# DeltaNet with a quick-GELU block: conversion steps, hops, Gram products and combinations of w_out in another order

## The chip, the cores and the metric

The kernel runs on one core of a Trainium2 chip. Its time is the device time of one execution in microseconds; the median of three runs is given. The engines are TensorE (PE, with its weight loads as PEld), VectorE (DVE), ScalarE (ACT), GpSimd (POOL) and SyncE (SP), whose queue issues most transfers. Each engine has its own instruction queue.

## The reference

```python
batch, n_heads, seq, head_dim = (4, 8, 768, 48)
n_tokens, d_model, d_ff = (3072, 384, 2048)

k_n = k / (np.linalg.norm(k, axis=-1, keepdims=True) + 1e-06)
state = np.zeros((B, H, D, D), dtype=np.float32)
for t in range(S):
    kt, vt, bt = (k_n[:, :, t], v[:, :, t], beta[:, :, t, None])
    y[:, :, t] = np.einsum('bhd,bhde->bhe', q[:, :, t], state)
    v_old = np.einsum('bhde,bhd->bhe', state, kt)
    state = state + bt[:, :, :, None] * np.einsum('bhd,bhe->bhde', kt, vt - v_old)

x = y.transpose(0, 2, 1, 3).reshape(B * S, H * D)
h = x @ w_in
g = h * (1.0 / (1.0 + np.exp(-1.702 * h)))
out = g @ w_out
```

`w_in` and `w_out` arrive as 64-bit floats; the kernel reads them as pairs of 32-bit words and makes 32-bit floats of them itself.

## The kernel before

**Units and chunks.** The sequence is cut into 6 chunks of 128 positions. A unit is one chunk of one batch with its 8 heads, so there are 24 units, numbered chunk by chunk: units 0 to 3 are chunk 0, units 4 to 7 (B to B + 3) chunk 1. Two units with the same chunk make a pair with one tile xT of 256 columns.

**A unit's own work.** For each unit the keys are normalized and transposed (`turn`, tile kT; psT is its PSUM tile), multiplied with themselves (`gram`, psG, tile G), and the diagonal blocks of 32 by 32 are sent through DRAM (`send_blocks`: tile Nd; `load_diagonal`: tile NT), so that one DVE routine, `invert`, inverts those of a whole chunk at once. The inverse comes back through DRAM as XB. Then the four blocks of a unit are solved one after another. `together` does one step of this for two units, a *hop*: for one unit `solve` (psU from XB and V on PE, copied by ACT to US), for the other `below` (psR from US and G on PE) and `rest`, in which DVE subtracts psR from V. A unit's next solve needs that subtraction, so hops alternate between PE, ACT and DVE. `queries`, `outputs` and `state` then make the unit's results (psY) and its new state ST; `put_out` calls them, copies psY to xT with ACT, and for the second unit of a pair moves the rows kept in `last` into xT by six transfers.

**Conversion.** `conversion` turns one piece of the 64-bit words into floats in five steps: a DVE step (`ts` on the high words) with an ACT step behind it, then a sign step, a step on the high words, a step on the low words and a product. `background()` strings all of them together: the 9 pieces of w_in, then `invert(1)`, the inverse of chunk 1, and then the 14 pieces of w_out, 23 pieces in all. `fill(us)` takes the next steps of this string, by costs written in the code, until the amount is used up. When a piece is done, `fetches` may start the load of a later one into the room that came free: the end of the second piece starts the last quarter of w_in (12 transfers), the end of the fourth starts w_out 4 to 7.

**Order.** Most instructions go through `pinned`, which keeps them in the order in which the program emits them, per engine and in SP's queue. Calls of `nc.gpsimd` and `nc.sync` that aren't pinned may be placed by the planner where the engine is free in its own estimate.

**Start of the program** (lines 1041 to 1187). Chunk 0's keys and inverse come first, then the masks of units 0 to 3 (`select`, POOL), then eight hops of units 0 and 1 with `fill(1.7)` behind each but the first, the Gram products of units 6 and 7 and their transfers, `put_out` of units 0 and 1, a list of transfers (the third, fourth and later loads of keys, the first three w_out pieces by `fetch_out`), then eight hops of units 2 and 3 with `fill(1.7)`, from the fourth on with a `feed()` each. `feed()` emits one step of `hidden`: three matmuls of x with w_in, or the last three of a pair of rows and the GELU on ACT (psum tile ph, result gT). After `put_out` of units 2 and 3, 25 rounds of `fill(1.0)` and `feed()` follow, in which `hidden` of the first two pairs ends.

**Main part.** `woven(n, share)` runs for each unit n from 3 on: solves for it, its follower and its forerunner, the preparation of a later unit (`normalize`, `prepare`), steps of a later inverse, and between them `spend`, which takes matmuls from a queue of FFN work. For the first pair that work is `both_written`, for the second `written`, and from the third on `hidden` and then `seven`, which multiplies gT with w_out by seven products of half size in place of eight. For that, four combinations of the quarters of w_out are needed:

```python
W11, W21 = w_out[:, 0:HF, 0:HM], w_out[:, HF:, 0:HM]
W12, W22 = w_out[:, 0:HF, HM:], w_out[:, HF:, HM:]
for o, a, b in ((T1, W12, W11), (T2, W22, T1), (T3, W22, W12), (T4, W21, T2)):
    for f in range(0, HF, n):
        add(o[:, f : f + n], a[:, f : f + n], b[:, f : f + n], sub_)
```

Each is four subtractions on POOL of 128 by 384 elements; `combined()` yields after each, 16 times. T3 takes the place of W12. T1, T2 and T4 lie in a tile TW of 4608 columns, 1536 each. Earlier TW holds other things: columns 0 to 2047 the later half of the second pair's gT (`late_g`, read by `written`), 2048 to 3071 queries of units 2 and 3 and then the mask of unit 5, 3072 to 3583 the keys KX of units 7 and 11, copied away in `follow(5)`. `follow(6)` queues `hidden` of the third pair, and `beside_of` takes one step of `combined()` before each of its 16 steps.

**Two rows that the prediction uses by name.** "rn" is the inverse key norm in `normalize`: POOL squares the keys (ksq), DVE sums them, POOL takes the root (rn), DVE adds a constant and inverts, POOL multiplies the keys (KN). The transposition of those keys (psT) is pinned in PE's order.

Of the kernel before, what the change touches and what calls it, by code (L numbers as in the profile page):

```python
# [18 lines left out]
def kernel(  # L19
# [21 lines left out]
    B, H, S, D = q.shape  # L41
# [9 lines left out]
    NB = C // BS  # L51
    HB = 2
    NTH = HB * C
    FQ = 4
    GB = 6
    HF, HM = FC // 2, DM // 2
# [22 lines left out]
    TW = cpool.tile([128, 3 * HF * HM], F32, name="TW")  # L79
# [10 lines left out]
    def load(n, pairs, dma=nc.sync.dma_start):  # L90
        c, b = units[n]
        for dst, src in pairs:
            dma(  # L93
                out=place(dst, n)[:, :, 0:D],
                in_=src[b, :, c * C : (c + 1) * C, :].rearrange("h p d -> p h d"),
            )

    def load_values(n, dma=nc.sync.dma_start):
        c, b = units[n]
        V = io.tile([128, H, D], F32, tag="V", name="V", bufs=4)  # L100
        dma(
            out=V, in_=v[b, :, c * C : (c + 1) * C, :].rearrange("h p d -> p h d")
        )
        loaded[n] = V
# [199 lines left out]
    def fill(us):  # L304
        while us > 0:
            us -= next(behind, us)
# [105 lines left out]
    def gram(n):  # L412

        c, b = units[n]
        kT = kTs[n]
        G = wk.tile([128, H, 128], F32, tag="G", name="G", bufs=6)
        pool_, tag = (ps_seq, "seq") if c == 0 else (ps_big, "big")
        ps = [pool_.tile([128, NP, 128], F32, tag=tag, name="psG") for _ in range(2)]
        for h in range(H):
            r = slice(h % 2 * 64, h % 2 * 64 + D)  # L420
            pe.matmul(
                ps[h % 2][:, h // 2], lhsT=kT[r, h // 2, :], rhs=kT[r, h // 2, :],
                start=True, stop=True,
            )
        act.activation(G[:, 0::2], ps[0], ACT.Copy)
        if B <= n < 2 * B + HB:
            act.activation(G[:, 1::2], ps[1], ACT.Copy)
        else:
            vec.tensor_copy(G[:, 1::2], ps[1])
        ready[n] = KN[n % len(KN)], kT, G  # L430
        return G
# [15 lines left out]
    def prepare(n):  # L447

        turn(n)
        yield 0.6  # L450
        gram(n)
        dma = sync if n < 3 * B else nc.sync.dma_start
        load_diagonal(n, send_blocks(n, dma=dma), dma)
        yield 0.9
# [6 lines left out]
    def send_blocks(n, others=(), dma=sync):  # L461

        G = ready[n][2]
        Nd = dram.tile([H * C * BS], F32, tag="Nd", name="Nd", bufs=4)
        to = Nd.rearrange("(h p k) -> p h k", p=C, k=BS)
        for blk in range(NB):
            u = slice(blk * BS, (blk + 1) * BS)
            (beside if blk in others else dma)(out=to[u], in_=G[u, :, u])
        return Nd

    def load_diagonals(Nds):

        for b in range(B):
            load_diagonal(b, Nds[b], sync)
# [90 lines left out]
    def bank(name, shape=(128, H, D)):  # L565
        return ps_seq.tile(list(shape), F32, tag="seq", name=name)
# [194 lines left out]
    def add(o, a, b, op, engine=None):  # L761
        (engine or nc.gpsimd).tensor_tensor(o, a, b, op=op)  # L762
# [1 line left out]
    W11, W21 = w_out[:, 0:HF, 0:HM], w_out[:, HF:, 0:HM]  # L764
    W12, W22 = w_out[:, 0:HF, HM:], w_out[:, HF:, HM:]
    T1, T2, T4 = (
        TW[:, i * HF * HM : (i + 1) * HF * HM].rearrange("p (f d) -> p f d", f=HF) for i in range(3)
    )
    T3 = W12

    def combined():

        n = 2
# [3 lines that stand above are left out]
                yield  # L777

    def beside_of(work, other):

        for cost in work:
            next(other, None)
            yield cost
        run(other)

# [108 lines left out]
    def take(cost):  # L894

        while cost > 0 and queue:
            more = next(queue[0], None)
            if more is None:
                queue.pop(0)
            else:  # L900
                cost -= more
                yield more

    def run(work):
        for _ in work:
            pass

    def ahead_of(work, n):
        for _ in range(n):
            next(work, None)  # L910
# [18 lines left out]
    def together(solves, belows):  # L929

        solves = [(X, blk) for X, blk in solves if X]
        belows = [(X, blk) for X, blk in belows if X]
        psU = bank("psU") if solves else None
        psR = bank("psR") if belows else None
        for h in range(H):
            for X, blk in solves:
                X.solve(blk, h, psU)
            for X, blk in belows:
                X.below(blk, h, psR)
        for X, blk in solves:  # L940
            X.solved(blk, psU)
        for X, blk in belows:
            X.rest(blk, psR)

    def follow(n):

        if n + 3 < len(units):
            load(n + 3, ((QP, q),))
        m = n - 1 + len(KN)
        if n == B + 1:  # L950
            nc.sync.dma_start(out=KN[m % len(KN)], in_=KX)
        elif n > B and m < len(units):
            load(m, ((KN, k),), nc.gpsimd.dma_start)
        if n - 1 + B < len(units):
            load_values(n - 1 + B)
        if n % HB == 0 and n > B:
            h = (n - 1) // HB
            gT, sums = [], []
            work = hidden(xTs[h], gT, slice(0, NTH), 1.3, sums)
            queue.append(beside_of(work, combined()) if h == HB else work)  # L960
            queue.append(seven(*units[h * HB], gT, sums))
            xTs.pop(h)

    debt = [0.0]

    def spend(cost):

        debt[0] = debt[0] + cost if queue else 0.0
        for done in take(debt[0]):
            debt[0] -= done  # L970
# [4 lines left out]
    def woven(n, share):  # L975

        nonlocal inverting  # L980
        A, B_, D_ = steps.pop(n - 1, None), steps.get(n), steps.get(n + 1) or NoStep()
        m = n + B + 1 if n > B else len(units)
        K = normalize(m) if m < len(units) and m >= 3 * B else iter(())
        P = prepare(m) if m < len(units) else iter(())
        if n == B:
            inverting = invert(*units[2 * B], HB)
        if n % HB == 1 and B + 1 < n and n + 1 + HB < len(units):
            inverting = invert(*units[n + 1 + HB], HB)
        ahead = FIRST[n] if n in FIRST else STEPS[:3] if n % HB == 1 else STEPS[3:]

        next(K, None)
        together([(B_, 1)], [(A, 2)])
        run(D_.scored)
        next(K, None)
        ahead_of(inverting, ahead[0])
        spend(share / 3)

        together([(A, 3), (D_, 0)], [(B_, 1)])
        next(K, None)
        ahead_of(inverting, ahead[1])  # L1000
        spend(share / 6)
        next(P, None)
        spend(share / 6)

        together([(B_, 2)], [(D_, 0)])
        if A:
            A.queries()
            A.outputs(True)
        run(P)
        ahead_of(inverting, ahead[2])  # L1010
        if n % HB == 0 and n > B:
            run(inverting)
        spend(share / 6)
        next(new_step(n + 2).scored, None)
        spend(share / 6)
        follow(n)

    queue = []
# [53 lines left out]
    pair = [new_step(n) for n in range(B)]  # L1072
# [11 lines left out]
    Ndx = [send_blocks(n) for n in (B, B + 1)]  # L1084
    run(scaling)
    pool.memset(late_U[:, H * D :], 0.0)
    for s in pair:
        s.select()

    def hops(a, b):  # L1090

        yield [(a, 0)], []
        for blk in range(NB - 1):
            yield [(b, blk)], [(a, blk)]
            yield [(a, blk + 1)], [(b, blk)]
        yield [(b, NB - 1)], []

    def put_out(s):
        s.queries()
        s.outputs(True, lambda: fill(1.7))  # L1100
        steps.pop(s.n)

    path = hops(*pair[:2])
    for i in range(2 * NB):
# [2 lines left out]
            turn(B + HB + i // 2)  # L1107
        if i > 0:
            fill(1.7)
    for n in (B + 2, B + 3):  # L1110
        gram(n)
        Ndx.append(send_blocks(n))
    load_diagonals(Ndx)
    for s in pair[:2]:
        put_out(s)
    sync(out=KN[0], in_=KX)
    load(8, ((KN, k),), sync)
    for f in range(3):
# [6 lines left out]
    def feed(n=1):  # L1125
        for _ in range(n):
            while ffn and next(ffn[0], None) is None:
                ffn.pop(0)

    gTs = [], []  # L1130
    ffn.append(hidden(xTs[0], gTs[0], slice(0, NTH), 1.3))
    path = hops(*pair[2:])
    for i in range(2 * NB):
        together(*next(path))
        if i > 2:
            feed()
        fill(1.7)
    for s in pair[2:]:
        put_out(s)
        feed()  # L1140
# [43 lines left out]
    queue = [both_written(0, gTs[0]), written(*units[HB], gTs[1])]  # L1184
# [34 lines left out]
```

## Time and profile before

| what | us |
|---|---|
| median of three runs | 775.18 (773.53 to 778.63) |
| the profiled execution's time | 778.5 |
| its span, first to last instruction | 776.8 |
| PE busy | 730.6 |
| DVE busy | 487.7 |
| ACT busy | 238.6 |
| POOL busy | 237.7 |

The profile is of one execution. All positions in this document are microseconds from the span's start. Most of the kernel's lines go through one helper, `pinned`, so nearly all rows carry its line number L108; they are told apart by tile names, "out<-in". "x4" is the number of instructions that a row merges. A bracket at a row's end is the engine's idle time before it and what ended it. PE's matmuls in 32-bit floats are two instructions each. In the table of busy shares by stretch, the stages around the edits read:

```profile
102.00:118.00 16.00, 16.00 (x200) 12.24 (x194) 12.58 (x25) 6.56 (x11) 0.00 (x0) 0.74 0.60 153
118.00:161.00 43.00, 42.61 (x263) 36.53 (x258) 40.75 (x87) 19.02 (x41) 8.12 (x5) 1.00 0.47 95
161.00:178.70 17.70, 14.09 (x99) 8.22 (x98) 16.26 (x34) 5.84 (x11) 0.00 (x0) 0.90 0.50 136
178.70:235.00 56.30, 55.51 (x789) 37.15 (x789) 44.22 (x94) 19.45 (x47) 14.01 (x13) 1.00 0.18 42
235.00:252.00 17.00, 12.45 (x119) 9.97 (x116) 13.34 (x32) 4.53 (x10) 12.18 (x11) 0.95 0.43 91
```

The columns are the stretch, its length, the busy time of PE, PEld, DVE, ACT and POOL with the number of instructions, the clock granted to PE as a share of the full one, the share of the transfer engines and GB/s. From 260 us to the end PE is busy almost without a break.

### The profile page before, as it was taken

What the parts mean: (1) busy time and instruction counts of PE and PEld (TensorE: products, weight loads), DVE (VectorE), ACT (ScalarE), POOL (GpSimd) and SP (SyncE); (2) the same over time, 40 slices, a digit from 0 to 9 for tenths busy, and PEclk for the clock granted to TensorE, in tenths of its full rate; (3) what the DMA queues carried; (4) which work ended last, traced back from release to release, by engine and by line L of the source; (5) the groups of instructions that cost most, each with busy time, mean ns of one, the idle gap of its engine ahead of it and who ended that gap; (6) DMA issues with size and microseconds to landing.
All of it is one profiled execution on the core that took longest, in us unless ns stands there. A gap on an engine that the chain in (4) does not pass through costs nothing.

```text
span 776.8 us, 19495 instructions
## 1 busy us (share of the span) xinstructions
PE 730.6 (94%) x8356; PEld 626.8 (81%) x8356; DVE 487.7 (63%) x1013; ACT 238.6 (31%) x527; POOL 237.7 (31%) x210
## 2 busy tenths in 40 slices
PE   8388789989997999999999999999999999999998
PEld 6266668856666898898898898888988988988988
DVE  4796689999768577687687687677677750120000
ACT  3363443533332322422323322322322313222120
POOL 5022001200057362352442542542620611403123
PEclk8576679999999899999999999999999999999999
DMA  9994654531224104104113113113113020000000
GB/s 169 123 173 100 169 127 82 123 102 50 59 46 84 35 13 95 38 19 92 35 25 84 35 27 84 35 31 79 36 23 77 20 56 2 2 27 1 26 1 21
DMA packets 128182, 47.11 MB, mean 61 GB/s; under 512 B 117920, under 2 KB 122144, under 8 KB 128096
## 3 DMA queue, kind: packets, MB, share of 16 engines
q1 hardware_dynamic: 125568, 41.54, 25.7%
q0 software_dynamic: 1344, 3.93, 2.2%
q8 instruction: 66, 1.08, 0.6%
q10 hardware_dynamic: 1184, 0.39, 0.2%
q14 instruction: 20, 0.16, 0.1%
HBM read 33.13 MB, written 11.01 MB: 57 GB/s over the span
## 4 chain that ended last, share of the span: by engine, by line
PE 74%; DVE 15%; DMA 4%; issue 3%; SPq 2%; POOL 2%; ACT 1%; DVEq 0%; POOLq 0%; ACTq 0%
PE ph L108 28%; PE po L108 25%; PE psY L108 5%; PE psU L108 5%; DVE P L108 4%; PE psG L108 4%; PE psQ L108 3%; DVE YB L108 3%; DVE w_out L108 2%; SPq L108 2%; PE psT L108 2%; PE psR L108 2%; DVE NT L108 2%; DMA w_out<-in_moe_w_in_dram 1%; DMA Nd<-G 1%
## 5 line engine op out<-in xcount | busy, mean ns | idle before, releaser
L108 PE MATMUL ph<-xT,w_in 128*128 128x256 f32 x1152 | 266.7, 387 | 0.4 <-DMA xT<-last 0.4
L108 PEld LDWEIGHTS ph<-xT,w_in 128*128 128x128 f32 x1152 | 217.6, 193 | 33.1 <-DVE V L108 1.4
L108 PE MATMUL po<-w_out,gT 128*128 128x192 f32 (+1 forms) x736 | 147.2, 354 | 4.0 <-DVE o L108 3.6
L762 POOL TENSOR_TENSOR gT<-gT 128x512 f32<-128x512 f32 x80 | 105.9, 1332 | 123.9 <-ACT gT L108 113.4
L108 DVE TENSOR_TENSOR V<-V,psR 64x384 f32<-64x384 f32 (+1 forms) x96 | 53.3, 556 | 135.5 <-PE psR L108 134.2
L108 PEld LDWEIGHTS po<-w_out,gT 128*128 128x128 f32 x736 | 121.2, 191 | 19.6 <-DVE o L108 4.6
L108 ACT ACTIVATE gT<-ph 128x512 f32<-128x512 f32 x92 | 54.9, 596 | 147.0 <-PE ph L108 146.9
L108 DVE TENSOR_TENSOR P<-NT,YB 64x2 f32<-64x2 f32 (+9 forms) x200 | 96.0, 480 | 6.2
L108 PEld LDWEIGHTS psU<-V,XB 32*32 32x32 f32 x1536 | 61.3, 109 | 33.6 <-issue 12.8
L108 DVE TENSOR_REDUCE YB<-P 64x2 f32<-64x2 f32 (+9 forms) x200 | 81.8, 409 | 6.9
L108 PE MATMUL po<-TW,gT 128*128 128x192 f32 x480 | 83.0, 328 | 0.0
L108 ACT COPY US<-psU 32x384 f32<-32x384 f32 x92 | 43.2, 469 | 128.5 <-PE psR L108 117.5
L108 PE MATMUL psU<-V,XB 32*32 32x48 f32 x1536 | 72.4, 208 | 9.4 <-DVE V L108 9.2
L108 PEld LDWEIGHTS po<-TW,gT 128*128 128x128 f32 x480 | 77.9, 190 | 1.1 <-issue 0.3
L108 PE MATMUL psR<-US,G 32*32 32x48 f32 x2208 | 63.7, 207 | 4.2 <-ACT US L108 4.1
L108 DVE TENSOR_TENSOR o<-o,po 128x192 f32<-128x192 f32 x40 | 13.5, 351 | 75.8 <-PE po L108 75.3
L108 PEld LDWEIGHTS psR<-US,G 32*32 32x32 f32 x2208 | 54.0, 108 | 5.6 <-ACT US L108 4.9
L631 POOL TENSOR_SCALAR_AFFINE_SELECT M<-M 128x1024 f32<-128x1024 f32 x19 | 22.3, 1173 | 94.3 <-DVE M L108 62.4
L108 DVE TENSOR_TENSOR P<-NT 64x512 f32<-64x512 f32 (+7 forms) x50 | 44.1, 883 | 2.4 <-DVE NT L108 0.5
L108 PE MATMUL psG<-kT 48*128 48x128 f32 x384 | 36.3, 335 | 1.3 <-ACT G L108 1.0
L93 POOL DMA_DIRECT2D KN<-in_k_dram x12 | 11.5, 958 | 84.1 <-PE psY L108 84.1
L108 PE MATMUL psQ<-QS,kT 48*128 48x176 f32 (+1 forms) x368 | 34.5, 330 | 0.8 <-ACT QS L108 0.8
(118 smaller groups left out, 735.7 us busy)
## 6 DMA issues: line engine op xcount, KB each, us to landing
V<-in_v_dram SPq DMA_DIRECT2D x24, 192.0 KB, 3.1
out_dram<-o SPq DMA_DIRECT2D x24, 192.0 KB, 2.1
QP<-in_q_dram SPq DMA_DIRECT2D x22, 192.0 KB, 3.3
raw<-in_moe_w_out_dram SPq DMA_DIRECT2D x9, 384.0 KB, 4.3
NT<-Nd SPq DMA_DIRECT2D x24, 128.0 KB, 2.9
XB<-Yd SPq DMA_DIRECT2D x24, 128.0 KB, 2.9
Nd<-G SPq DMA_DIRECT2D x92, 32.0 KB, 1.8
Yd<-NT SPq DMA_DIRECT2D x22, 128.0 KB, 2.2
```

Of the source, the lines that this page charges most:

```text
L93: dma(out=place(dst, n)[:, :, 0:D], in_=src[b, :, c * C : (c + 1) * C, :].rearrange("h p d -> p h d"),)
L108: return lambda *a, **kw: tc.keep_in_program_order(op(*a, **kw))
L631: (pool if self.n < B else nc.gpsimd).affine_select(out=self.M, in_=self.M, compare_op=ALU.is_gt, fill=0.0, base=0, pattern=[[0, H], [1, 1 ...
L762: (engine or nc.gpsimd).tensor_tensor(o, a, b, op=op)
```

## The change

Four edits. The areas of T1 and T4 in TW change places, and T1's four subtractions are emitted in `woven(6)`, while those of T2, T3 and T4 stay beside the fifth and later steps of `hidden`. `fill(5.5)` comes between the masks of chunk 0 and its first hop. The first two hops of units 2 and 3 move up: each is followed by `fill(1.0)`, the Gram product of unit 6 or 7 with its transfers, `put_out` of unit 0 or 1 and another `fill(1.0)`; the loads of the diagonals now come behind all of this. The other six hops of units 2 and 3 have `fill(2.3)` instead of `fill(1.7)`; feeds begin at the same hop as before.

```diff
     T1, T2, T4 = (
-        TW[:, i * HF * HM : (i + 1) * HF * HM].rearrange("p (f d) -> p f d", f=HF) for i in range(3)
+        TW[:, i * HF * HM : (i + 1) * HF * HM].rearrange("p (f d) -> p f d", f=HF) for i in (2, 1, 0)
     )
...
     def beside_of(work, other):
 
-        for cost in work:
-            next(other, None)
+        for i, cost in enumerate(work):
+            if i >= FQ:
+                next(other, None)
             yield cost
         run(other)
...
-            queue.append(beside_of(work, combined()) if h == HB else work)
+            queue.append(beside_of(work, combining) if h == HB else work)
...
+    combining = combined()
     debt = [0.0]
...
         next(P, None)
+        if n == B + HB:
+            ahead_of(combining, HF // 2)
         spend(share / 6)
...
     for s in pair:
         s.select()
+    fill(5.5)
...
-    for n in (B + 2, B + 3):
-        gram(n)
-        Ndx.append(send_blocks(n))
+    path = hops(*pair[2:])
+    for i in range(HB):
+        together(*next(path))
+        fill(1.0)
+        gram(B + HB + i)
+        Ndx.append(send_blocks(B + HB + i))
+        put_out(pair[i])
+        fill(1.0)
     load_diagonals(Ndx)
-    for s in pair[:2]:
-        put_out(s)
     sync(out=KN[0], in_=KX)
     load(8, ((KN, k),), sync)
     for f in range(3):
         fetch_out(f)
...
-    path = hops(*pair[2:])
-    for i in range(2 * NB):
+    for i in range(HB, 2 * NB):
         together(*next(path))
-        if i > 2:
+        if i > HB:
             feed()
-        fill(1.7)
+        fill(2.3)
```

`put_out` contains a fill of its own, between the products of the new state and the addition to ST:

```python
def put_out(s):
    s.queries()
    s.outputs(True, lambda: fill(1.7))
    steps.pop(s.n)
```

## The prediction

> **What bounds the kernel now.** I read the busy slices of the page first, then the timelines of VectorE (DVE), SyncE's queue (SP), GpSimd (POOL) and TensorE (PE) around the edited places, last the chain of waits from 234 us on. The slices (19.4 us each):
>
> ```profile
> PE   8388789989997999999999999999999999999998
> DVE  4796689999768577687687687677677750120000
> PEclk8576679999999899999999999999999999999999
> ```
>
> PE is near full from 110 us on and DVE until 190 us; both are loose between 60 and 110 us, and later PE itself dips in the thirteenth slice and its clock in the fourteenth (233 to 272 us). The edits touch just these two places. DVE's timeline of the first:
>
> ```profile
> 61.99 0.55 DVE L108 TENSOR_TENSOR TW<-TW 128x384 f32<-128x384 f32 x1
> 69.08 1.14 DVE L108 TENSOR_TENSOR V<-V,psR 32x384 f32<-32x384 f32 x2 [6.54 <-PE psR L108]
> ...
> 93.28 0.36 DVE L108 TENSOR_TENSOR ST<-psY,ST 128x192 f32<-128x192 f32 x1 [5.24 <-PE psY L108]
> ...
> 111.91 0.34 DVE L108 TENSOR_SCALAR w_out<-raw 128x384 int32<-128x384 int32 x1
> ```
>
> Two holes, 6.54 and 5.24 us, are to be filled. The last line is the first step of the first w_out piece; what it reads comes late in SP's queue:
>
> ```profile
> 94.37 1.80 SPq L108 DMA_DIRECT2D NT<-Nd  x4
> 96.22 4.94 SPq L108 DMA_DIRECT2D xT<-last  x6
> 101.26 0.54 SPq L108 DMA_DIRECT2D KN<-TW  x1
> 101.90 0.54 SPq L108 DMA_DIRECT2D KN<-in_k_dram  x1
> 102.49 1.65 SPq L108 DMA_DIRECT2D raw<-in_moe_w_out_dram  x3
> ```
>
> ```profile
> DMA to landing us min/median/max: 4.0/4.5/5.2
> ```
>
> So raw lands at 102.5 + 4.5 = 107, 5 us before DVE asks. The second place, first POOL's timeline, then the chain of waits:
>
> ```profile
> 223.76 1.68 POOL L762 TENSOR_TENSOR TW<-w_out 128x384 f32<-128x384 f32 x1 [3.74 <-PE po L108]
> ```
>
> ```profile
> 239.54 5.80 POOL TW L762 x5
> 245.34 1.05 POOL M L631
> 246.39 1.63 POOL rn L325
> 248.01 2.65 issue
> 250.70 1.01 POOL KN L329
> 251.76 1.11 PE psT L108 x4
> 252.88 6.00 PE ph L108 x18
> ```
>
> POOL's first combination waits 3.74 us for PE to read the TW area it overwrites; the 16 combinations end at 245.3, and the key normalization behind them holds PE for 4.19 us (its idle time before that psT). The 18 ph instructions then take 6.00 us, against 3.89 for 18 at 266.1: the clock has fallen to half.
>
> **Steps behind the masks.** Going through the costs of the generators, `fill(5.5)` emits seven steps. Priced by the starts of the same kinds at 70.2 to 76.6 (0.61, 0.59, 0.94, 1.83 for two, 0.61, 0.68) they are 5.3 us: 62.5 to 67.8, inside the first hole. The seventh also queues a 0.94 us ACT step (row at 71.55) ahead of the first hop's copy of U. That copy ran at 67.62; it now starts at about 68.8, and the hops 1.2 us later. The second piece's end releases twelve fetches of the last w_in quarter; SP reaches them behind the eight Nd stores at 71.9 instead of 74.6. DVE wants them at 88; hidden. The w_out fetches 4 to 7 follow the second quarter's end likewise, some 6 us sooner, and nobody waits.
>
> **Pair 1's first sets between Gram products and outputs.** DVE's work on chunk 0's first eight hops is the same 17 steps, on smaller pieces (512 for 768 columns), until about 86.7. Then fills of 1.0, 1.7 and 1.0 stand around each Gram product and output; the second hole is gone. PE's work is the one it had. In after's order I get, with PE at half clock: Gram 6 until 89, outputs of unit 0 until 92, first receiving hop 94, Gram 7 until 95.5, outputs of unit 1 until 98.5, next hop's subtractions until 101.6. Before, the same subtractions ended at 101.1. So the hops are not sooner, but DVE has eight more steps behind it (0.69, 0.95, 0.6, 0.6, 0.94, 0.92, 0.91, 0.61 = 6.2 us).
>
> **The new wait.** The next step in after's order, at once after those subtractions, is the first w_out step, which stood three hops later. Its fetch did not move up: in SP's queue it now stands behind the four stores of Gram 7, the six xT moves, the four NT loads and the two KN moves. Gram 7's copies wait on ACT behind a conversion step until 98.4; then four stores (1.8 at 160.6, 2.9 as half of eight at 88.4) to 100.2 to 101.3; six xT moves 3.7 (124.1) to 4.94; four NT 1.8; KN twice 0.6. The raw fetch goes at 107 to 109 and lands 4.0 to 4.5 later: 111 to 113, I take 112. (The NT loads land by 109, and the inverse needs them at 115: hidden, as long as raw is later.) DVE stands from 101.6 to 112, 10 us, and queued behind it are the subtractions of four hops, so PE stands too. The w_out step starts when it did before (111.9), but with hops 4 to 7 and their five feeds of `hidden` still to come.
>
> Then 0.34 + 0.95 + 0.96, a subtraction 0.57, and hops with fills of 2.4, 2.5 and 2.2 us (inverse steps at 114.6 to 122.9) and 0.57 each: the last subtraction ends at 123.6, unit 2's outputs start 2.1 later (0.75 hop, 1.3 feed) at 125.7. At half clock a hop with its feed took 4.28 us (102.23 to 106.51) instead of 3.0, and after PE's thin work at 94 to 102 the half clock lasted into two such hops: up to 2.6 more, 128.3. Against 116.64 that is +9.1 to +11.7; I take +10. From there PE has the list it had at 118 to 161, busy 42.6 of 43.0 us, so `hidden` ends at 171.
>
> [...]
>
> The stretch 161 to 178.7 is held by DVE (16.3 of 17.7 us busy, PE 14.1). After, DVE reaches its end, the subtraction at 177.4, later by 2.5 (the 0.7 and three subtractions owed) and by the conversions now ahead of it (178.6 to 182.95 and 187.9 to 190.5: 7.0): 186.9. PE would be there at 171 + 13.5 = 184.5. So +9. What DVE then lacks wins little: PE is busy 55.5 of 56.3 us from 178.7 to 235. I take **+8.5**. Bounds: landing at 108 gives +4, landing at 113.5 with half clock in all hops +12.
>
> **First combination sooner, area swapped.** Four subtractions, 1.0 each (225.5 to 229.6), go to an area whose last reader is the KX copy, so they fit into the 3.74 us before 223.76. With the areas swapped, only two pieces of the second and two of the fourth combination still wait for PE's last TW reads (233.2); after that I count four pieces instead of eight, each about 1.1, so POOL ends at 240.7 instead of 245.3. But the rn step on DVE, at 250.21, is also in order behind inverse steps. Those were slowed: five operations at 240.61 to 246.4 took 1.96, 0.84, 0.74, 0.74, 0.82 beside POOL; with POOL idle the first took 1.21 (183.61), the second 0.15 (184.86) and later ones 0.17; the one beside a POOL mask at 185.23 took 0.77. Undisturbed DVE gains 2.5 to 3.2, and psT starts at 248.6 to 249.3, with a stall of 1.0 to 1.7 instead of 4.19: −2.8. A stall that short cost no clock at 293.3 (1.19); the 18 ph and the psT then save 2.1 + 0.6. Together **−5**, bounds 0 and −7.
>
> [...]
>
> **Sum.** The profiled execution has a span of 776.8 and a time of 778.5, 3.3 over the median of 775.18. 776.8 + 8.5 − 5 = 780.3; on the median, 778.7: **779 us**. A change under 1% (7.75 us) is about what a measurement here can tell from none.
>
> **Rivals.** *POOL's head start is worth nothing* (slower). If DVE reaches rn at 250 whatever POOL does, because it waits until 240.61 for the NT load and the planner places the unpinned combinations as before, the −5 falls away: 775.2 + 8.5 = 784. It decides once DVE's rn starts after 249.5. For it: DVE had been ready for rn 2.2 us later than POOL. Against: the slowed operations. With the larger first bounds this case reaches 787.
>
> *The raw fetch is in time* (faster). If SP gets there before 98, or DVE is that much slower, the wait is gone: DVE keeps the two holes, 6.2, PE the saved half clock at 100 to 110 (4): −9 − 5 = 761. Against: 12 us of SP issues and landing lie between the xT copies and raw, and DVE has 2.7 us of work there.
>
> *The conversions bring nothing, and no new wait either*, because PE has its work to do from 110 on: only −5, 770. It needs a wait half as long, so it lies inside the forecast's lower end.
>
> **How the numbers follow.** Forecast (a small loss left by +8.5 and −5; its own range 770 to 783) 0.45 with the third rival in it; slower rival and larger losses 0.38; faster rival 0.17. These are also the chances of within 1%, slower and faster. The range leaves out a tenth at each end: 764 to 787.
>
> **What would show it.** Right: a DVE idle time of 8 to 12 us ended by the raw fetch near 112, no idle of 6.5 at 62; unit 2's psY near 127; ph of `hidden` ending near 171; POOL's combinations ending near 240.7 plus the shift of 8.5, and a psT stall under 2 us at full clock. Wrong: w_out's first step starting before 105, or the inverse near 103; then the loss is a gain. If the hops catch up after 112 without costing PE, the first term was mis-sized.

## The result and the profile after

The changed kernel takes 786.3 us (median of four runs, 785.73 to 788.86). The kernel before, run beside it on the same chip, takes 776.9 (773.53 to 778.69). The ratio is 1.0133 with a 95% interval of 1.0085 to 1.018: slower by 1.3%. The profiled execution took 786.8 with a span of 785.1, where the profiled execution of before had a span of 776.8.

The busy slices of the changed kernel, to be held against the three rows of before (19.6 us each):

```profile
PE   8286829899999999999999999999999999999998
DVE  4798849988866676676587687687686760110000
PEclk9575659999999999999999999999999999999999
```

The clock's dip in the fourteenth slice is gone, and so is PE's. The price stands in the sixth slice (98 to 118 us): PE fell from 8 to 2, DVE from 8 to 4. VectorE's timeline shows both places where the early part went another way than forecast:

```profile
59.95 0.55 DVE L108 TENSOR_TENSOR TW<-TW 128x384 f32<-128x384 f32 x1
...
61.02 1.49 DVE L108 TENSOR_SCALAR w_in<-w_out 128x768 int32<-128x768 int32 x1
62.44 1.57 DVE L108 SCALAR_TENSOR_TENSOR w_out<-w_out 128x768 f32<-128x768 uint32 x1
64.05 3.48 DVE L108 SCALAR_TENSOR_TENSOR w_in<-w_out,w_in 128x768 f32<-128x768 f32 x2
...
68.17 0.68 DVE L108 TENSOR_SCALAR w_in<-w_out 128x768 int32<-128x768 int32 x1
71.78 1.14 DVE L108 TENSOR_TENSOR V<-V,psR 32x384 f32<-32x384 f32 x2 [2.93 <-PE psR L108]
...
101.89 1.14 DVE L108 TENSOR_TENSOR V<-V,psR 32x384 f32<-32x384 f32 x2
113.64 0.36 DVE L108 TENSOR_SCALAR w_out<-raw 128x384 int32<-128x384 int32 x1 [10.61 <-DMA raw<-in_moe_w_out_dram]
```

The last row is the wait that the prediction named: 10.61 us, at the first w_out step, at once behind the subtractions. The rows above it are the seven steps at the masks. Four of them take 1.7 to 2.2 times what the same shapes took in before at 70 to 76 us (1.49 for 0.68, 1.57 for 0.94, 3.48 for 1.83 for two), so the seven last from 60.42 to 68.85, 8.4 us instead of 5.3, and the first subtraction comes 11.83 us behind the TW row instead of 7.09 (61.99 to 69.08 in before). POOL's timeline shows its masks beside them:

```profile
60.88 4.08 POOL L108 TENSOR_SCALAR_AFFINE_SELECT M<-M 128x1024 f32<-128x1024 f32 x3
64.92 1.80 POOL L108 TENSOR_SCALAR_AFFINE_SELECT TW<-TW 128x1024 f32<-128x1024 f32 x1
```

The masks last from 60.88 to 66.72. The first of the seven steps starts before them and the last two after them; these three took 0.68, 0.69 and 0.68 us (0.68 to 0.69 in before). ScalarE's timeline shows what stands between the steps and the first subtraction:

```profile
68.88 0.93 ACT L108 ACTIVATE w_in<-w_in,low 128x768 int32<-128x768 int32 x1 [5.40 <-DVE w_in L108]
69.72 0.45 ACT L108 COPY US<-psU 32x384 f32<-32x384 f32 x1
```

ACT waited 5.40 us for the last of the seven DVE steps, and the first copy of U is queued behind the step that this wait holds up. SP's queue explains the wait for raw:

```profile
92.07 9.70 SPq L108 DMA_DIRECT2D Nd<-G  x8
101.87 3.78 SPq L108 DMA_DIRECT2D xT<-last  x6
105.74 1.91 SPq L108 DMA_DIRECT2D NT<-Nd  x4
107.75 0.54 SPq L108 DMA_DIRECT2D KN<-TW  x1
...
108.98 1.65 SPq L108 DMA_DIRECT2D raw<-in_moe_w_out_dram  x3
```

It is the order that the prediction read from the code, and raw goes at 108.98 (forecast 107 to 109; the yardstick below makes this agreement smaller). The second place, in POOL's timeline and then in a stretch of the chain of waits:

```profile
163.65 1.65 POOL L762 TENSOR_TENSOR TW<-w_out 128x384 f32<-128x384 f32 x1 [0.46 <-DVE w_out L108]
...
170.80 1.29 POOL L762 TENSOR_TENSOR TW<-w_out 128x384 f32<-128x384 f32 x1
...
236.03 2.07 POOL L762 TENSOR_TENSOR TW<-w_out 128x384 f32<-128x384 f32 x2 [0.56 <-PE psT L108]
```

```profile
252.12 1.05 POOL M L631
253.16 2.60 POOL rn L325
255.77 4.12 issue
...
259.92 1.01 POOL KN L329
...
260.98 0.88 PE psT L108 x4
261.86 5.35 PE ph L108 x18
```

The first combination is spread over 163 to 238 us. POOL's mask comes at 252.12. PE's idle time before this psT is 1.91 us (4.19 before).

**A yardstick.** The two profiled executions don't start alike. Up to the masks no edit changes anything, yet the last product of chunk 0's inverse (the DVE row NT<-YB,bI, 1.61 us ahead of the TW row above) starts at 60.38 in before and at 58.34 in after. So below, positions are taken relative to that product, at three later points: the first subtraction V<-V,psR; the new state of unit 5, the DVE row ST<-psY at 210.15 in before, 221.50 in after; and the state in before's row at 403.82, behind the second place.

| profiled execution | product | first V, behind it | unit 5's state, behind it | against before | from there to the later state |
|---|---|---|---|---|---|
| before | 60.38 | 8.70 | 149.77 | | 193.67 |
| after | 58.34 | 13.44 | 163.16 | +13.4 | 190.64 |
| e1_raw_early | 57.47 | 13.46 | 158.86 | +9.1 | 190.30 |
| e2_raw_and_diagonals | 57.32 | 13.45 | 156.95 | +7.2 | 188.77 |
| e3_first_area_only | 61.40 | 8.37 | 149.55 | −0.2 | 188.88 |
| e4_steps_only | 60.09 | 13.46 | 155.32 | +5.6 | 192.81 |
| e5_regrouped_only | 57.39 | 8.30 | 153.06 | +3.3 | 192.45 |
| e6_no_masks | 58.09 | 9.72 | 160.74 | +11.0 | 188.42 |
| e7_no_steps_at_masks | 57.23 | 8.47 | 152.28 | +2.5 | 188.88 |
| e8_four_steps | 57.87 | 8.29 | 148.16 | −1.6 | 188.93 |
| e9_smaller_fills | 61.48 | 13.03 | 157.75 | +8.0 | 189.06 |
| e10_regrouped_four_steps | 59.49 | 8.26 | 151.32 | +1.6 | 190.10 |

Each row is one execution. Where medians were taken, the two differences of a row together agree with the change of the medians within 2.6 us (at worst in e8_four_steps: −6.3 by the rows, −3.7 by the ratio); differences of a microsecond or two between rows are not shown by the times.

For after against before the columns add up: −2.0 at the start, +13.4 in the early part, −3.0 between the two states make +8.4; the spans differ by 8.3.

### The profile page after: what moved, and what is told of

It reads as the page before. It is cut to its first block, busy times and chain, and to the rows that moved or that the text cites. A ratio compares the mean times of both kernels' runs of the same rounds, so it can differ in the third digit from the quotient of the medians.

```text
span 785.1 us, 19495 instructions
## 1 busy us (share of the span) xinstructions
PE 724.2 (92%) x8356; PEld 620.9 (79%) x8356; DVE 489.2 (62%) x1013; ACT 237.8 (30%) x527; POOL 243.0 (31%) x210
## 4 chain that ended last, share of the span: by engine, by line
PE 72%; DVE 13%; DMA 4%; issue 3%; SPq 3%; POOL 2%; ACT 1%; DVEq 0%; POOLq 0%; ACTq 0%
PE ph L108 27%; PE po L108 26%; PE psY L108 5%; PE psU L108 5%; DVE P L108 4%; PE psQ L108 3%; SPq L108 3%; DVE YB L108 3%; PE psG L108 2%; PE psR L108 2%; PE psT L108 2%; DVE w_out L108 1%; DVE NT L108 1%; DMA KN<-in_k_dram 1%; POOL TW L762 1%
## 5 line engine op out<-in xcount | busy, mean ns | idle before, releaser
L108 PEld LDWEIGHTS po<-w_out,gT 128*128 128x128 f32 x736 | 120.6, 190 | 19.6 <-DVE o L108 4.6
L108 DVE TENSOR_TENSOR P<-NT,YB 64x2 f32<-64x2 f32 (+9 forms) x200 | 93.4, 467 | 6.3
L108 PE MATMUL psU<-V,XB 32*32 32x48 f32 x1536 | 74.0, 211 | 17.4 <-DVE V L108 16.6
L108 DVE TENSOR_TENSOR o<-o,po 128x192 f32<-128x192 f32 x40 | 13.5, 351 | 75.8 <-PE po L108 75.3
L108 POOL TENSOR_TENSOR rn<-ssq,half 128x8 f32<-128x8 f32 x4 | 7.8, 1940 | 95.8 <-DVE ssq L108 95.8
L108 DVE TENSOR_REDUCE NT<-P 64x32 f32<-64x512 f32 (+9 forms) x50 | 33.4, 668 | 1.7
```

The costliest lines, as they stand in the source:

```text
L108: return lambda *a, **kw: tc.keep_in_program_order(op(*a, **kw))
```

## The experiments

Theory 1 in the expectations below is that the wait for raw makes the early loss; theory 2 that the order on DVE and ACT does, with an inverse or conversion steps ahead of copies that PE needs; theory 3 that the first hops are late because the steps at the masks run slowly beside POOL.

**The raw fetch early.** One of the three fetches moves ahead of the hops:

```diff
     fill(5.5)
+    fetch_out(0)
...
-    for f in range(3):
+    for f in range(1, 3):
         fetch_out(f)
```

> The changed kernel with one edit: the fetch of the first w_out piece goes into SP's queue right behind the conversion steps at the masks, long before it is asked for. Theory 1 (the wait for that fetch is the main cost): the 10.6 us idle of DVE before the first w_out step is gone; DVE is next held some 4 us by the NT loads, which in the changed kernel are issued at 105.7 and land near 110 while the inverse would be asked for near 106. Time 5 to 7 us below the changed kernel, near 780. Theory 2 (the order itself costs: inverse and conversions stand in front of the GELU copies on DVE and ACT, and PE waits for those): the idle of DVE goes, but PE stands longer for the GELU copies later, and the time stays within 3 us of the changed kernel. Theory 3 (the first hops are late, because the steps at the masks run slowly beside POOL): the first subtraction of psR still comes 13 us after the inverse's last product, against 8.7 in the kernel before, so 4 to 5 us of the loss stay whatever the fetch does.

780.86 us, ratio to before 1.005 (1.0028 to 1.0072). The DVE timeline of this run:

```profile
102.00 0.36 DVE L108 TENSOR_SCALAR w_out<-raw 128x384 int32<-128x384 int32 x1
...
108.88 1.23 DVE L108 TENSOR_TENSOR NT<-NT,bI 128x1024 f32<-128x1024 f32 x1 [4.06 <-DMA NT<-Nd]
```

The first w_out step has no idle time any more, and 4 us later DVE stands again, for the diagonals that chunk 1's inverse needs. The prediction had called them hidden "as long as raw is later"; raw no longer is. Unit 5's state gains 4.3 us. A wait of 10.61 us was worth less than half of its length, in part because the next transfer in the same queue was late as well.

**The diagonals early too.** In addition, the loads of the diagonals go ahead of the outputs of unit 1:

```diff
+        if i == HB - 1:
+            load_diagonals(Ndx)
         put_out(pair[i])
         fill(1.0)
-    load_diagonals(Ndx)
```

> The same, and the NT loads go into SP's queue ahead of the second output's xT moves. Theory 1: no idle of DVE over 2 us between 100 and 116 us; the inverse starts near 106 instead of 116.5; time 9 to 11 us below the changed kernel, 775 to 777, about the time of the kernel before. Theory 2: the inverse starts 10 us sooner, and at most 3 us of it reach the end of the program. Theory 3: the time stays 4 to 5 us above what the early start promises, near 780.

779.19 us, ratio 1.0028 (1.0009 to 1.0047). The wait for NT shrinks from 4.06 to 1.21 us and unit 5's state gains another 1.9. So the waits that theory 1 speaks of are 6.2 of 13.4 us; the first hops are still 4.7 us late, and 7.2 us remain. The time stays above the 775 to 777 that theory 1 alone gave.

**The combinations alone.** Before, with only the swapped areas and the sooner first combination:

```diff
-        TW[:, i * HF * HM : (i + 1) * HF * HM].rearrange("p (f d) -> p f d", f=HF) for i in range(3)
+        TW[:, i * HF * HM : (i + 1) * HF * HM].rearrange("p (f d) -> p f d", f=HF) for i in (2, 1, 0)
...
+        if n == B + HB:
+            ahead_of(combining, HF // 2)
```

> The kernel before with the edits of the combinations alone (areas of the first and the fourth swapped, first one emitted sooner). From the two traces (the shift of PE's list is 11.4 us before that place and 8.3 behind it): 3 us faster than the kernel before, psT waits 1.5 to 2.5 us for the keys instead of 4.2. If the gain in the changed kernel came from its later place and not from these edits: no difference, within 1 us.

773.33 us, ratio 0.996 (0.9938 to 0.9982). Its chain of waits:

```profile
241.72 2.07 POOL M L631
243.79 1.63 POOL rn L325
...
249.30 1.02 POOL KN L329
...
250.36 0.66 PE psT L108 x4
251.02 3.89 PE ph L108 x18
```

The 18 ph take 3.89 us in the chain against 6.00 in before, PE's stall is 1.69, and from state to state 4.8 us are won: the term of −5, nearly whole, in the profiles. The medians give less, 3.1 us (1.4 to 4.8), and the next two runs, whose combinations are those of before, take 192.81 and 192.45 us from state to state, so up to 1.2 us of the 4.8 may not belong to this edit. In after 3.0 of it are left; there the stall was 1.91 and the 18 ph took 5.35, with a granted clock of 0.83 over 260 to 270 us.

**The steps at the masks alone.** Before, with only this edit:

```diff
     for s in pair:
         s.select()
+    fill(5.5)
```

> The kernel before with the conversion steps at the masks alone. Theory 3: the seven steps take 8 us instead of 5.3 beside POOL's masks, the first hop's copy of U waits behind the seventh step's ACT operation, and the first subtraction of psR comes 13 us after the inverse's last product instead of 8.7; the first w_out step is asked for three hops sooner, waits 3 to 6 us for its fetch, and the time is 4 to 7 us over the kernel before. Theory 1 alone: the hops start within 1.5 us of where they did, DVE waits 3 to 6 us at the first w_out step, and the time is 0 to 3 us over the kernel before.

782.92 us, ratio 1.0075 (1.0048 to 1.0103). The first subtraction is 4.8 us late, as in after (4.7), and DVE waits only 2.26 us for raw. This edit, which was priced as filling a hole, alone costs 5.6 us at unit 5's state.

**The regrouping alone.** Before, with only the moved hops, Gram products and outputs (after, without the steps at the masks and with the combinations as in before):

```diff
+    for i in range(HB):
+        together(*next(path))
+        fill(1.0)
+        gram(B + HB + i)
+        Ndx.append(send_blocks(B + HB + i))
+        put_out(pair[i])
+        fill(1.0)
...
-        fill(1.7)
+        fill(2.3)
```

> The kernel before with the regrouping of the hops, Gram products and outputs alone (no steps at the masks, old areas of the combinations). Theory 1 (the wait for the first w_out piece): DVE reaches that step in the fourth hop of units 2 and 3, near 106, and waits some 5 us; counted from the inverse's last product, the state of unit 5 comes 6 to 8 us later than in the kernel before (149.8 us after it there, 163.2 in the changed kernel), and the time is 6 to 8 us over the kernel before. If regrouping costs only where the steps at the masks have run ahead: no wait over 2 us, and 0 to 2 us over the kernel before.

778.76 us, ratio 1.0024 (0.9999 to 1.0048). The first subtraction is on time, DVE waits 6.53 us for raw at 108.30, and unit 5's state is 3.3 us late. The parts alone give +5.6 and +3.3; together they give 13.4. The longer wait of after comes from a later fetch and not from a sooner DVE: counted from the product, DVE is ready for the first w_out step at 44.4 us here and at 44.7 in after (one hop sooner in the program, but behind hops that are late), while raw is issued at 45.8 here and at 50.6 in after, behind Gram products and outputs that follow those hops.

**The masks away.** After, without the four masks of chunk 0 on POOL: the kernel leaves them out and computes the products that use them from unmasked values; the instructions of the other engines are the same:

```diff
-    for s in pair:
-        s.select()
     fill(5.5)
```

> The changed kernel without the four masks of chunk 0 on POOL (the results of chunk 0 then hold terms that the masks remove). Theory 3 (POOL's masks slow the DVE steps beside them): the second to fifth of the seven steps fall from 1.5 to 1.75 us each to 0.7 to 0.95, the seven take 5.3 us in place of 8.4, and the first subtraction of psR comes 10 to 10.5 us after the inverse's last product instead of 13.4. If the steps are slow for another reason (transfers into their words, for one): no change in either. The time is no test here, as DVE waits for the first w_out piece anyhow.

781.92 us in a single run. DVE's timeline, for the same rows as in after:

```profile
60.77 0.68 DVE L108 TENSOR_SCALAR w_in<-w_out 128x768 int32<-128x768 int32 x1
61.36 0.94 DVE L108 SCALAR_TENSOR_TENSOR w_out<-w_out 128x768 f32<-128x768 uint32 x1
62.34 1.83 DVE L108 SCALAR_TENSOR_TENSOR w_in<-w_out,w_in 128x768 f32<-128x768 f32 x2
...
67.81 1.14 DVE L108 TENSOR_TENSOR V<-V,psR 32x384 f32<-32x384 f32 x2 [2.32 <-PE psR L108]
```

0.68, 0.94 and 1.83: the seven steps take 5.3 us, just as they had been priced, and the first subtraction is 1.0 us late (forecast 1.2). So it is POOL's masks that make these steps slow. The wait for raw stays (10.33 us), and raw is issued and landed some 4 us sooner behind the product. Unit 2's outputs (the first psY behind the wait, at 116.64 in before, 128.12 in after and 123.75 here) come 9.4 us later behind the product than in before, where after's come 13.5 later; at unit 5's state the difference is 2.4 us.

**No steps at the masks, fetches early.** The second kernel above without its steps at the masks:

```diff
-    fill(5.5)
     fetch_out(0)
```

> The second experiment (early fetch of the first w_out piece, early NT loads) without the conversion steps at the masks. Theory 3: the first subtraction is back at 8.7 us after the inverse's last product, and the state of unit 5 comes 5 us sooner than there (157.0), at 151 to 152; time 773 to 776. Theory 2 (inverse and conversions ahead of the GELU copies): PE still waits 3 to 5 us for GELU copies between 118 and 160 us. If regrouping gains once nothing stands in its way: state of unit 5 before 148, time under 772.

774.51 us, ratio 0.9971 (0.9943 to 0.9999). The first subtraction is on time and unit 5's state comes 4.7 us sooner than in the second kernel: nearly the whole lateness of the first hops (5.0 us between the two) arrives at the state. What the regrouping costs with its transfers early is the remaining 2.5 us.

**Four steps at the masks, no regrouping.** The combinations alone, with a smaller amount at the masks and the early fetch:

```diff
     for s in pair:
         s.select()
+    fill(3.0)
+    fetch_out(0)
...
-    for f in range(3):
+    for f in range(1, 3):
         fetch_out(f)
```

> The kernel before with the combinations' edits, an early fetch of the first w_out piece, and four steps at the masks instead of seven (so none that puts an ACT operation in front of the first hop's copy; about 5.4 us beside POOL, inside the hole of 6.5). Theory 3: the first subtraction is within 0.3 us of the kernel before (8.7 after the inverse's last product); DVE is 3.3 us of work ahead from there on; time 770 to 773, up to 3 us under the experiment with the combinations' edits alone (773.3). If DVE's lead wins nothing because PE bounds the rest: 773 to 774.

771.62 us, ratio 0.9952 (0.9922 to 0.9982). DVE's timeline:

```profile
60.55 1.49 DVE L108 TENSOR_SCALAR w_in<-w_out 128x768 int32<-128x768 int32 x1
61.97 1.57 DVE L108 SCALAR_TENSOR_TENSOR w_out<-w_out 128x768 f32<-128x768 uint32 x1
63.58 1.73 DVE L108 SCALAR_TENSOR_TENSOR w_in<-w_out,w_in 128x768 f32<-128x768 f32 x1
66.16 1.14 DVE L108 TENSOR_TENSOR V<-V,psR 32x384 f32<-32x384 f32 x2 [0.86 <-PE psR L108]
```

The steps are as slow as in after, but four of them end at 65.3, no second ACT step is queued ahead of the copy of U, and DVE still waits 0.86 us for PE. The hole is filled without delay, and unit 5's state comes 1.6 us sooner than in before. This is the fastest kernel of the study, below both versions. That it also beats the combinations alone (773.33) the times don't show: the two ran on different chips, and their intervals overlap.

**The regrouping with four steps.** The second kernel with a smaller amount at the masks:

```diff
-    fill(5.5)
+    fill(3.0)
     fetch_out(0)
```

> This is e2_raw_and_diagonals with an allowance of 3.0 in place of 5.5 at chunk 0's masks, so four steps in place of seven there. Theory 3 (the first hops are late because seven steps run slowly beside POOL's masks): the first subtraction V<-V,psR is within 1 us of before's 8.7 us behind the last product of chunk 0's inverse, and unit 5's state, 156.95 behind it in e2 and 152.28 in e7 without any steps there, comes to 150 to 152.5; the time is 773 to 775, a ratio of about 0.996. Rival (the regrouping itself, with its fills between Gram products and outputs, costs some 2.5 us that no step at the masks changes): unit 5's state stays 2 to 4 us behind that of e8_four_steps (148.2), whose first hops are the same. Rival 2 (it is the mere amount of conversion work in front, not its place): four steps done early save as many later and the state is at 148 as in e8, the time 771 to 772.

775.59 us, ratio 0.999 (0.9963 to 1.0016). First hops as in the run before this one, and unit 5's state 3.2 us behind it: the rival of this experiment holds beside theory 3, and rival 2, which wanted the state at 148, falls. In the profiles the regrouping itself costs some 2.5 to 3.2 us that neither the steps nor the two late transfers explain.

**Smaller fills behind the hops.** The second kernel with less work behind the last six hops of units 2 and 3, because PE's waits for the GELU copies (gT) were the largest left between 118 and 161 us. In after, the list of what PE waited for from 100 to 185 us begins:

```profile
PE psU L108 <- DVE V L108: 12.6, 3, 7.9
PE ph L108 <- ACT gT L108: 4.5, 2, 3.3
```

The columns are the sum, the number of waits and the longest. The first row is the wait for raw as PE sees it, through the subtractions that stood behind it on DVE; the second is aimed at here.

```diff
-        fill(2.3)
+        fill(1.7)
```

> This is e2_raw_and_diagonals with allowances of 1.7 in place of 2.3 behind the last six hops of units 2 and 3, so that fewer steps of the second inverse stand on DVE ahead of ACT's conversion steps and the GELU copies. Theory 2 (PE's waits for GELU copies come from the order on DVE and ACT): the waits of PE for gT between 130 and 155 us, 4.5 us in e1 and e2, fall under 2, and unit 5's state comes 1.5 to 3 us sooner behind the last product of chunk 0's inverse than 156.95; time 776 to 778. Theory 3 alone: the waits go only when the first hops come sooner, so the state stays at 156 to 158 and the time at 779.

779.61 us, ratio 1.0025 (1.0004 to 1.0045). In the same list of this run:

```profile
PE po L108 <- ACT TW L108: 2.3, 1, 2.3
PE ph L108 <- ACT gT L108: 1.9, 2, 1.4
```

The waits for gT fell from 4.5 to 1.9 us as expected, but the wait for TW grew from 0.8 (in the second kernel) to 2.3, and unit 5's state is 0.8 us later, not sooner. Theory 2 fits the waits for gT, which fall with the fills, and is wrong about what they are worth. Why nothing is won isn't shown; DVE has the same steps to do, and PE waits for other work later.

## Why the prediction was wrong

**The direction.** Two terms of opposite sign were to leave a small loss within 1%; the loss is 1.3%, though the time of 786.3 lies inside the range given, 764 to 787. The mechanisms named are there, and the early term was mis-sized: +8.5 forecast with bounds of +4 to +12, +13.4 measured against the yardstick, beyond its upper bound.

**Steps behind the masks: the step that failed.** "Priced by the starts of the same kinds" they were "5.3 us: 62.5 to 67.8, inside the first hole", and the hops 1.2 us late. They took 8.4 us and the first hops were 4.7 late. The rows used as prices stood where POOL was idle (0.00 us busy from 70 to 77 us in before). Without the masks the forecast holds (5.3 and 1.0), and beside them four steps fit without delay where seven didn't. The prediction itself cites slowed DVE rows beside POOL for the second place (1.96 for 1.21 us, 0.84 for 0.15); it didn't ask who else was on POOL at 62 us, where the masks stand in the line above the edit. Three of the four slowed steps read two inputs, among them the one that reads the high and the low words of one tile (1.57 for 0.94); the fourth reads one tensor and slowed most (1.49 for 0.68). No run shows by what means the masks slow them.

What this step of the forecast cost is read from after against the run without masks, where the steps took the time that the prediction gave them: 4.1 us at unit 2's outputs (+13.5 against +9.4) and 2.4 us at unit 5's state (+13.4 against +11.0). Leaving the steps out of the second kernel wins 4.7 us there.

**The new wait.** Why, where and how long were right: 10.61 us (forecast 10) at the step and behind the queue that it named. That the positions agree too, raw issued at 108.98 (forecast 107 to 109) and unit 2's outputs at 128.12 (forecast 128.3), is in part luck, as this execution of after started 2.0 us sooner. Counted from the product, raw was issued at 50.6 us, where the forecast's 107 to 109 are 46.6 to 48.6 on before's clock. In the run without masks it was issued at 46.8, and the outputs of unit 2 came 9.4 us late (forecast 9.1 to 11.7): with the steps priced rightly the path holds up to there. What the wait is worth by itself isn't its length: taking it away wins 6.7 us at unit 2's outputs and 4.3 at unit 5's state, with the diagonals behind it 6.2. Taken away in the order of the runs, the 13.4 us are 4.3 raw, 1.9 the diagonals, 4.7 the steps at the masks and 2.5 the regrouping; since the parts alone add up to 8.9, another order would share them out differently.

**"`hidden` ends at 171": a second step that failed.** Its last ph ran at 176.2 to 177.8 (the clock positions as they are; 2 us more on the yardstick), although the outputs of unit 2 came at 128.12. The step assumed that PE, "busy 42.6 of 43.0 us" there, would be so again. In after it was busy 38.34 of these 43 us:

```profile
102.00:118.00 16.00, 5.89 (x103) 4.57 (x103) 5.19 (x9) 1.08 (x2) 0.00 (x0) 0.50 0.71 187
118.00:161.00 43.00, 38.34 (x294) 31.50 (x295) 38.34 (x82) 16.43 (x32) 2.55 (x1) 0.96 0.38 76
```

A list that was full behind a punctual DVE isn't full behind a late one: 4.5 us went to waits for GELU copies. The smaller fills reduced these waits without bringing unit 5's state sooner, so they are not by themselves the loss. The forecast let +10 at unit 2's outputs shrink to +8.5. In after 13.5 stayed 13.4, and in the run without masks, with the same waits of 4.5 us, 9.4 grew to 11.0. Of the 4.9 us between +8.5 and +13.4 at unit 5's state, 2.4 are thus the slow steps, and 2.5 are there without them; where exactly these arise stays open.

**Conversions done early.** "What DVE then lacks wins little" fits: four steps done in time, with the early fetch, move unit 5's state by 1.4 us in the profiles (−1.6 against −0.2), and the times don't tell it from nothing.

**Combinations.** The size of −5 (its own parts, 2.8 and 2.7, add up to 5.5) came out as −4.8 alone and −3.0 in after, by the profiles. POOL's last combination was to end at 240.7 plus the shift; it ended at 252.1, which less the shift of 11.35 us at unit 5's state is 240.8. The stall was 1.69 and 1.91 (forecast 1.0 to 1.7). The statement that a short stall costs no clock held alone and not in after, where the 18 ph took 5.35 us instead of 3.89. The stall's length alone doesn't decide it: over the nine profiles with these edits the stall is 1.15 to 1.92 us, the 18 ph take 3.89 us in six of them and 5.35 to 5.58 in three, and e1_raw_early and e9_smaller_fills have the same stall of 1.92 us with 5.57 us (a granted clock of 0.50 from 257 to 259 us) and 3.89 us (1.00 from 259 to 263). So some 1.5 us of this term may differ between executions of one kernel; with one profile each, that stays open. The first four subtractions didn't run at 225 to 230 together: the planner set two of them at 163 and 171 and left two until PE's psT had read their room (236.03); the end was the same.

**The rivals.** "POOL's head start is worth nothing" ended on the side that the result took, but its mechanism isn't what happened: DVE's rn started at 259.43, which less the shift is 248.1, before the 249.5 at which it was to decide. That the time fell there is luck. "The raw fetch is in time" was refuted at 113.64, and where the fetch was made early (first experiment) the kernel was still slower than before, so even that case was worth far less than the 761 us it was given. The third rival needed a wait half as long.

**What stays open.** Where within the regrouping its own 2.5 to 3.2 us lie, and whether the times would confirm their size. With four steps, PE is idle or waiting 2.2 us more than without the regrouping over the 146 us from the TW row on; the last experiment speaks against the waits for gT.

## What to carry to other kernels

Price a step that is moved from rows that had the same neighbours: a look at what POOL does in the place it is moved to would have shown the masks, beside which four of DVE's steps cost 1.7 to 2.2 times as much. Leave slack when a hole is filled: four steps ending before the hole did delayed nothing, seven ending after it made the first hops 4.7 us late. A wait that is seen and measured isn't yet the loss: with it gone, the next transfer in the same queue took part of its place, and a 10.6 us wait was worth 4.3. And compare positions from a point behind the program's start: counted from the start, forecasts here seemed to hold that were 2 us off.

## What the runs showed beyond this

The program's start, which no edit touches, doesn't always take the same time. The Gram products of the first units run at half clock in some profiled executions and at full clock in others (0.50 and 1.00 granted over the two rows below). One unit's products on PE, first in before, then in after:

```profile
17.58 2.08 PE L108 MATMUL psG<-kT 48*128 48x128 f32 x16
```

```profile
16.15 1.16 PE L108 MATMUL psG<-kT 48*128 48x128 f32 x16
```

The granted clock over 14 to 24 us is 0.53 in the one and 0.92 in the other. Over the twelve profiles the last product of chunk 0's inverse starts at 57.2 to 58.3 us in the seven with a clock of 0.92 or more in that stretch, at 60.1 to 61.5 in the four with 0.59 or less, and at 59.5 in the one with 0.83. These 4 us are as much as most terms of this study; without the yardstick above, the early part would have read as +11.35 us and not +13.4. Why the granted clock differs there from one execution to the next, no run shows.

POOL's masks, too, take longer beside DVE's steps: three of them took 4.08 us in after, beside the conversion steps, and 3.19 in before, where those steps don't stand there.
